# Layer scale on one core: gamma in 16 GpSimd transfers and 16 small matmuls instead of one ScalarE-queue transfer and one matmul

## The chip, the core and the metric

The kernel runs on one core of a Trainium2 chip. The metric is the device time of one execution in microseconds; the figure to compare is the median of several runs. Beside it stands one profiled execution, with a page of readings and a trace that can be asked for more. The kernel is written in Bass: each engine has its own list of instructions, and all order between engines is made by semaphores that the kernel sets and waits for.

## The reference

```python
B, S, D = 1024, 16, 512
x, y: (B, S, D) bfloat16;  gamma: (D,) bfloat16

def reference(x, y, gamma):
    return x + gamma * y
```

The two inputs and the output are 16.8 MB each. Gamma is a single row of 512 numbers, 1 KB, which is applied to every row of y.

## The kernel before, in words

The 16,384 rows of 512 numbers are laid over 128 partitions, 128 consecutive rows to a partition. "Row" below means one of these 128 rows, over all partitions: 1 KB in each partition. All of y stays in SBUF (`y_sb`, 128 rows), and the result is written over it; x has a smaller buffer (`x_sb`, 75 rows), part of which is used twice.

The lists at the top of the file (L6 to L18) are the whole schedule, written by hand:

- `SP` is the list of loads that SyncE issues, in order: y rows 0 to 3, y rows 4 to 63, x rows 0 to 63, y rows 64 to 127, x rows 64 to 116, x rows 117 to 127. The fourth number of an x entry is its place in `x_sb`. Rows 64 to 116 go to the place of rows 0 to 52, so their load has to wait until the add that reads rows 0 to 52 is done (`frees`, L85, and the wait at L107). Rows 117 to 127 need no wait of their own, but stand behind that load in SyncE's list.
- `ACT` is the list of ScalarE's queue: gamma (`'g'`), then the two stores, rows 0 to 63 and rows 64 to 127.
- `EARLY` says that the first two of SyncE's loads are moved to the very start of the program.
- `DVE` is VectorE's order of work on four pieces of 53, 11, 53 and 11 rows: multiply 0, multiply 1, add 0, add 1, multiply 2, multiply 3, add 2, add 3. A multiply (L156) is `y_sb = y_sb * gamma`, an add (L165) is `y_sb = x_sb + y_sb`.

Gamma has to be on all 128 partitions. It is loaded as one row on one partition (`gamma_row`, L56 and L110), a matmul with a row of 128 ones (`ones_row`, L57) as the stationary operand spreads it to 128 partitions in PSUM (`gamma_ps`, L130), and VectorE copies it from there to `gamma_sb` as bfloat16 (L132). TensorE waits for the ones and for gamma ahead of the matmul; VectorE waits for the matmul ahead of the copy, and its first multiply comes after the copy and after y rows 4 to 63 have landed.

TensorE has one more duty: after the matmul it waits for the load of x rows 64 to 116 (`RELEASE`) and then signals `s_go` and `s_rel` (L135 to L137). ScalarE issues the first store only after `s_go`, so the stores begin when that load is in; the first store also needs adds 0 and 1, the second adds 2 and 3. At the end SyncE waits for all stores (L171).

`_take(sem, n, eng)` (L22 to L25) makes an engine wait until a semaphore has reached n and then lowers it by n. Waits that go through it are listed in the profile under L25.

Of the kernel before, what the change touches and what calls it, by code (L numbers as in the profile page):

```python
# [7 lines left out]


SP = [('y', 0, 4), ('y', 4, 64), ('x', 0, 64, 0), ('y', 64, 128), ('x', 64, 117, 0), ('x', 117, 128, 64)]  # L10
ACT = [('g',), ('s', 0, 64), ('s', 64, 128)]

EARLY = (2, 0)

# [7 lines left out]
def _take(sem, n, eng):  # L22


    return eng.wait_ge(sem, n).then_inc(sem, -n)  # L25


def kernel(
# [9 lines left out]
    nc = tc.nc  # L38
# [7 lines left out]
    N, D = xf.shape  # L46
# [4 lines left out]
    dt = xf.dtype  # L51
# [1 line left out]
    yv = yf.rearrange("(p n) d -> p n d", p=P)  # L53
    ov = of.rearrange("(p n) d -> p n d", p=P)

    gamma_row = nc.alloc_sbuf_tensor("gamma_row", [1, D], dt).ap()  # L56
    ones_row = nc.alloc_sbuf_tensor("ones_row", [1, P], dt).ap()  # L57
    gamma_sb = nc.alloc_sbuf_tensor("gamma_sb", [P, D], dt).ap()
    y_sb = nc.alloc_sbuf_tensor("y_sb", [P, rows, D], dt).ap()
    x_loads = [w for w in SP + ACT if w[0] == "x"]  # L60
    y_loads = [w for w in SP + ACT if w[0] == "y"]
    stores = [w for w in SP + ACT if w[0] == "s"]
    for loads in (x_loads, y_loads, stores):
# [3 lines left out]
    gamma_ps = nc.alloc_psum_tensor("gamma_ps", [P, D], mybir.dt.float32).ap()  # L67

    sem = nc.alloc_semaphore
    s_gamma, s_ones, s_ps, s_dve = sem("s_gamma"), sem("s_ones"), sem("s_ps"), sem("s_dve")  # L70
# [8 lines left out]
    def pieces_of(a, b):  # L79
        return [c for c in range(n) if meets(starts[c], starts[c + 1], a, b)]  # L80

    def x_at(row):
        return next(w[3] + row - w[1] for w in x_loads if w[1] <= row < w[2])

    def frees(w):  # L85

        c = set()
        for v in x_loads[: x_loads.index(w)]:
            lo, hi = max(v[3], w[3]), min(v[3] + v[2] - v[1], w[3] + w[2] - w[1])
            if lo < hi:  # L90
                c |= set(pieces_of(v[1] + lo - v[3], v[1] + hi - v[3]))
        return sorted(c)
# [3 lines left out]
    def ring(eng, what, n_early):  # L96

        known, went = 0, False
        for k, w in enumerate(what):
            kind = w[0]  # L100
            need = frees(w) if kind == "x" else pieces_of(w[1], w[2]) + list(w[3:]) if kind == "s" else []
            need = max((order[c] + 1 for c in need), default=0)
            if kind == "s" and not went:
                _take(s_go, 1, eng)
                went = True
            if need > known:
                eng.wait_ge(s_add, need)  # L107
                known = need
            if kind == "g":
                i = eng.dma_start(out=gamma_row, in_=gamma.unsqueeze(0)).then_inc(s_gamma, 16)  # L110
            elif kind == "x":
                to = x_sb[:, w[3] : w[3] + w[2] - w[1], :]
                i = eng.dma_start(out=to, in_=xv[:, w[1] : w[2], :]).then_inc(s_load[w], 16)
            elif kind == "y":
                r = slice(w[1], w[2])
                i = eng.dma_start(out=y_sb[:, r, :], in_=yv[:, r, :]).then_inc(s_load[w], 16)
            else:
                r = slice(w[1], w[2])
                i = eng.dma_start(out=ov[:, r, :], in_=y_sb[:, r, :]).then_inc(s_out, 16)
            if k < n_early:  # L120
                early.append(i.ins)

    ring(nc.sync, SP, EARLY[0])
    ring(nc.scalar, ACT, EARLY[1])


    nc.vector.memset(ones_row, 1.0).then_inc(s_ones, 1)  # L127
    _take(s_ones, 1, nc.tensor)
    _take(s_gamma, 16, nc.tensor)
    nc.tensor.matmul(gamma_ps, ones_row, gamma_row, start=True, stop=True).then_inc(s_ps, 1)  # L130
    _take(s_ps, 1, nc.vector)
    nc.vector.tensor_copy(out=gamma_sb, in_=gamma_ps).then_inc(s_dve, 1)  # L132
    _take(s_dve, 1, nc.vector)
# [16 lines left out]
    for kind, *args in DVE:  # L150
        c = args[0]
        yt = y_sb[:, starts[c] : starts[c + 1], :]
        if kind == "m":
            need(y_loads, c)
            g = gamma_sb[:, None, :].to_broadcast([P, PIECES[c], D])
            nc.vector.tensor_tensor(out=yt, in0=yt, in1=g, op=MULT).then_inc(s_dve, 1)  # L156
            open_mults += 1
        else:
# [4 lines left out]
            at = x_at(starts[c])  # L163
# [46 lines left out]
```

## Time and profile before

| | before |
|---|---|
| median of 3 runs (lowest to highest) | 120.06 us (119.98 to 120.09) |
| profiled execution: span from the first to the last instruction | 118.7 us |
| difference of the median to that span | 1.36 us |
| moved by DMA | 50.33 MB, mean 424 GB/s over the span |
| VectorE busy | 70.0 us, 59% of the span, 10 instructions |
| TensorE busy | 0.6 us, 1 matmul of 577 ns, 1 weight load of 99 ns |
| GpSimd busy | 0.2 us, 4 memsets at the start |
| large multiply or add (53 rows) | 14.29 us each |
| small multiply or add (11 rows) | 3.08 us each |

The trace gives the profiled execution's span and no separate device time for it, so the sums are made against the span of 118.7 us, and the 1.36 us between it and the median are carried over.

How to read it: the engines' busy times don't count the issuing of DMAs, waits and signals; these are seen in the timeline, where a name with a q (SPq, ACTq, PEq) is the sequencer that feeds an engine. A transfer is not in an engine's row at all once it is issued: it is seen in the DMA view, as packets of a queue. Queue q1 holds what SyncE issues, q10 what ScalarE issues. Each of the core's 16 DMA engines works on all the queues.

### The profile page before, as it was taken

The numbers are of one execution on the slowest core, as the hardware profiler recorded it, in microseconds if no ns is written. First come the engines' busy times: TensorE is split into PE (matmuls) and PEld (weight loads), VectorE is DVE, ScalarE is ACT, GpSimd is POOL, SyncE is SP. The second block draws the span as 40 slices with busy tenths as digits, with TensorE's granted clock in tenths as the row PEclk, the third lists the DMA queues.
The fourth block names the chain that finished last, engine by engine and source line by source line (L and its number), as shares of the span: only waits on it lengthen the run. The fifth ranks groups of instructions, "written<-read, shape, count | busy, mean of one in ns | idle before, by whom it ended". The sixth has DMA issues, their size and how long they took to land. (4 is left out here: it accounts for less than half of the span.)

```text
span 118.7 us, 80 instructions
## 1 busy us (share of the span) xinstructions
PE 0.6 (0%) x1; PEld 0.1 (0%) x1; DVE 70.0 (59%) x10; POOL 0.2 (0%) x4
## 2 busy tenths in 40 slices
PE   0001000000000000000000000000000000000000
PEld 0000000000000000000000000000000000000000
DVE  0002000599999299999759999999999910000000
POOL 0000000000000000000000000000000000000000
DMA  8977977998899888998896969498899889988891
GB/s 268 571 332 331 663 331 331 596 464 353 353 486 574 353 353 353 640 420 353 353 585 293 585 293 585 205 634 353 353 596 464 353 353 420 640 353 353 353 663 44
DMA packets 1154, 50.33 MB, mean 424 GB/s; under 512 B 129, under 2 KB 130, under 8 KB 258
## 3 DMA queue, kind: packets, MB, share of 16 engines
q1 hardware_dynamic: 864, 33.55, 66.0%
q10 hardware_dynamic: 290, 16.78, 32.6%
HBM read 33.56 MB, written 16.78 MB: 424 GB/s over the span
## 5 line engine op out<-in xcount | busy, mean ns | idle before, releaser
L156 DVE TENSOR_TENSOR y_sb<-y_sb,gamma_sb 128x27136 bf16<-128x27136 bf16 (+1 forms) x4 | 34.6, 8688 | 12.3 <-DVEq L25 12.3
L165 DVE TENSOR_TENSOR y_sb<-x_sb,y_sb 128x27136 bf16<-128x27136 bf16 (+1 forms) x4 | 34.6, 8689 | 2.3 <-DVEq L25 2.2
L132 DVE CAST gamma_sb<-gamma_ps 128x512 bf16<-128x512 f32 x1 | 0.7, 692 | 8.8 <-DVEq L25 8.8
L127 DVE MEMSET ones_row<- 1x128 bf16 x1 | 0.2, 165 | 2.0 <-PEq L41 2.0
L130 PE MATMUL gamma_ps<-gamma_row,ones_row 1*128 1x512 bf16 x1 | 0.6, 577 | 10.2 <-PEq L25 10.2
L130 PEld LDWEIGHTS gamma_ps<-gamma_row,ones_row 1*128 1x128 bf16 x1 | 0.1, 99 | 10.2 <-issue 10.2
L194 POOL MEMSET const-bfloat16-1.0<- 128x1 bf16 x1 | 0.1, 101 | 0.0
L194 POOL MEMSET const-uint8-127<- 128x1 uint8 x1 | 0.1, 101 | 0.0
L194 POOL MEMSET const-float32-0.0<- 128x1 f32 x1 | 0.1, 98 | 0.2 <-issue 0.2
L194 POOL MEMSET const-float32-1.0<- 128x1 f32 x1 | 0.1, 98 | 0.0
## 6 DMA issues: line engine op xcount, KB each, us to landing
y_sb<-in_y_dram SPq DMA_DIRECT2D x1, 7680.0 KB, 21.4
x_sb<-in_x_dram SPq DMA_DIRECT2D x1, 6784.0 KB, 20.8
x_sb<-in_x_dram SPq DMA_DIRECT2D x1, 1408.0 KB, 23.8
y_sb<-in_y_dram SPq DMA_DIRECT2D x1, 512.0 KB, 3.8
out_dram<-y_sb ACTq DMA_DIRECT2D x2, 22.8
x_sb<-in_x_dram SPq DMA_DIRECT2D x1, 39.3
gamma_row<-in_gamma_dram ACTq DMA_DIRECT2D x1, 1.0 KB
y_sb<-in_y_dram SPq DMA_DIRECT2D x1, 58.3
```

Of the source, the lines that this page charges most:

```text
L127: nc.vector.memset(ones_row, 1.0).then_inc(s_ones, 1)
L130: nc.tensor.matmul(gamma_ps, ones_row, gamma_row, start=True, stop=True).then_inc(s_ps, 1)
L132: nc.vector.tensor_copy(out=gamma_sb, in_=gamma_ps).then_inc(s_dve, 1)
L156: nc.vector.tensor_tensor(out=yt, in0=yt, in1=g, op=MULT).then_inc(s_dve, 1)
L165: nc.vector.tensor_tensor(out=yt, in0=xt, in1=yt, op=ADD).then_inc(s_add, 1)
L194: nc = _bacc.Bacc("TRN2", target_bir_lowering=False, num_devices=1)
```

## The change

Gamma leaves ScalarE's list. GpSimd issues 16 transfers instead, whose lengths are 16 different primes that add up to 512 (`GAMMA`); each has a semaphore of its own, and their destinations lie 96 elements apart in a longer `gamma_row`. GpSimd waits for all 16, signals `s_gamma` once, and then resets the state of these semaphores and clears them. TensorE waits for that one signal and spreads gamma with 16 matmuls, one for each piece, into the matching columns of `gamma_ps`; the last one signals VectorE. All else stays.

```diff
-ACT = [('g',), ('s', 0, 64), ('s', 64, 128)]
+ACT = [('s', 0, 64), ('s', 64, 128)]
+GAMMA = [67, 61, 59, 53, 47, 41, 37, 31, 29, 23, 19, 17, 13, 7, 5, 3]
+APART = 96
...
-    gamma_row = nc.alloc_sbuf_tensor("gamma_row", [1, D], dt).ap()
+    assert sum(GAMMA) == D
+    gamma_row = nc.alloc_sbuf_tensor("gamma_row", [1, len(GAMMA) * APART], dt).ap()
...
-            if kind == "g":
-                i = eng.dma_start(out=gamma_row, in_=gamma.unsqueeze(0)).then_inc(s_gamma, 16)
-            elif kind == "x":
+            if kind == "x":
...
     nc.vector.memset(ones_row, 1.0).then_inc(s_ones, 1)
     _take(s_ones, 1, nc.tensor)
-    _take(s_gamma, 16, nc.tensor)
-    nc.tensor.matmul(gamma_ps, ones_row, gamma_row, start=True, stop=True).then_inc(s_ps, 1)
+    pieces, sems = [], [sem(f"s_gamma_{k}") for k in range(len(GAMMA))]
+    for k, m in enumerate(GAMMA):
+        at = sum(GAMMA[:k])
+        pieces.append((at, m, gamma_row[:, k * APART : k * APART + m]))
+        nc.gpsimd.dma_start(out=pieces[k][2], in_=gamma[at : at + m].unsqueeze(0)).then_inc(sems[k], 16)
+    for s in sems:
+        nc.gpsimd.wait_ge(s, 16)
+    nc.gpsimd.sem_inc(s_gamma, 1)
+    nums = range(sems[0].num, sems[-1].num + 1)
+    assert [s.num for s in sems] == list(nums)
+    nc.gpsimd.dma_reset(nums)
+    nc.gpsimd.sem_clear(nums)
+    _take(s_gamma, 1, nc.tensor)
+    for at, m, piece in pieces:
+        i = nc.tensor.matmul(gamma_ps[:, at : at + m], ones_row, piece, start=True, stop=True)
+    i.then_inc(s_ps, 1)
     _take(s_ps, 1, nc.vector)
     nc.vector.tensor_copy(out=gamma_sb, in_=gamma_ps).then_inc(s_dve, 1)
```

## The prediction

> **What bounds the kernel now.** I read the page first: its row of slices and its queues, and the chain that ended last.
>
> ```profile
> DMA  8977977998899888998896969498899889988891
> q1 hardware_dynamic: 864, 33.55, 66.0%
> q10 hardware_dynamic: 290, 16.78, 32.6%
> HBM read 33.56 MB, written 16.78 MB: 424 GB/s over the span
> ```
>
> The DMA engines are busy in every slice: 50.33 MB at 424 GB/s are 118.7 us, the whole span. Queue 1 is SP's loads, queue 10 is ACT's gamma and stores. The kernel is bound by transfers, and time is lost only if the engines run dry. The chain that ended last is mostly "issue" and says no more, so I went to the timeline, to see which transfer waits for which compute.
>
> ```profile
> 1.91 0.52 ACTq L110 DMA_DIRECT2D gamma_row<-in_gamma_dram  x1
> 10.21 0.10 PEld L130 LDWEIGHTS gamma_ps<-gamma_row,ones_row 1*128 1x128 bf16 x1 [10.21 <-issue]
> 10.24 0.58 PE L130 MATMUL gamma_ps<-gamma_row,ones_row 1*128 1x512 bf16 x1 [10.24 <-PEq L25]
> 10.97 0.69 DVE L132 CAST gamma_sb<-gamma_ps 128x512 bf16<-128x512 f32 x1 [8.81 <-DVEq L25]
> 21.99 17.29 DVE L156 TENSOR_TENSOR y_sb<-y_sb,gamma_sb 128x27136 bf16<-128x27136 bf16 x2 [10.33 <-DVEq L25]
> 41.46 17.29 DVE L165 TENSOR_TENSOR y_sb<-x_sb,y_sb 128x27136 bf16<-128x27136 bf16 x2 [2.17 <-DVEq L25]
> 55.78 0.81 SPq L113 DMA_DIRECT2D x_sb<-in_x_dram  x2
> 60.69 17.29 DVE L156 TENSOR_TENSOR y_sb<-y_sb,gamma_sb 128x27136 bf16<-128x27136 bf16 x2 [1.94 <-DVEq L25]
> 76.95 18.85 ACTq L119 DMA_DIRECT2D out_dram<-y_sb  x2
> 78.13 17.30 DVE L165 TENSOR_TENSOR y_sb<-x_sb,y_sb 128x27136 bf16<-128x27136 bf16 x2
> ```
>
> Gamma is spread by 11.66 us (10.97 + 0.69), and the first multiply starts at 21.99 because y rows 4 to 63 land then. So gamma has 10.3 us to spare. Past that, the first add waits 2.17 us for x. At 55.75 (41.46 + 14.29, one large add) that add frees the space of x rows 64 to 116, and SP issues their load at 55.78. In the answer for 59 to 61 us its first packets move at 59.65, behind y's last ones. A load issued onto free engines moves after about 1.0 us (y's first four rows: issued at 0.00); the first store, beside a load, took up to 2.1 us. I take 1.5, so this load can be issued 59.65 - 55.78 - 1.5 = 2.4 us later for nothing. **Gamma may thus be ready as late as 21.99 + 2.17 + 2.4 = 26.6 us**; each microsecond beyond delays the load, then the release of the stores (which waits for that load), then the end.
>
> Next: why does a 1 KB transfer issued at 1.91 arrive only by 10.2? The DMA view of single microseconds, 7 to 8 and 9 to 10:
>
> ```profile
> DMA packets 17, 0.98 MB, mean 984 GB/s; under 512 B 0, under 2 KB 1, under 8 KB 1
> q1 hardware_dynamic: 16, 0.98, 226.7%
> q10 hardware_dynamic: 1, 0.00, 0.3%
> ...
> DMA packets 12, 0.68 MB, mean 676 GB/s; under 512 B 1, under 2 KB 1, under 8 KB 1
> q1 hardware_dynamic: 11, 0.68, 155.9%
> q10 hardware_dynamic: 1, 0.00, 0.1%
> ```
>
> The loads move in waves of 16 packets, one per engine, each 61,440 bytes (7680 KB in 128 packets); 4 to 5, 6 to 7 and 8 to 9 us start none. Gamma's data goes in the wave of 7 to 8 (narrower stretches: 7.3 to 7.5), its semaphore write only in the next, 9.6 to 9.8. **A small packet of another queue gets one turn after each big packet of the load queue.** A turn costs one wave: 0.983 MB at 430 GB/s (the rate from 22.0 to 41.5) is 2.28 us; the later loads' packets of 65,536 bytes make it 2.44.
>
> **What the Trainium skill says.** "DMA: Bandwidth & Descriptors", section "Queues, rings and completion order": a DMA engine takes turns between its queues packet by packet; the trace agrees, with 2.3 us between the two packets above. Same page, "Why a DMA increments its semaphore by 16 and not by 1": a transfer issued by SP or ACT has only the engines it uses post a semaphore write, but one issued by GpSimd has all 16 engines post one, whatever its shape. For ACT the trace agrees (290 packets = 256 of the stores, their 32 semaphore writes, and 2 of gamma); for GpSimd nothing here shows it. Same page, "Anatomy of one DMA — SWDGE (gpsimd) path": about 2.0 us fixed for each, mostly completion; not shown here.
>
> **The change, part by part.**
>
> Removed: one issue on ACT (0.52 us) and two small packets of one engine (0.3% and 0.1% of 16 engine-microseconds, some 0.06 us). ACT's next work waits until 76.95, so the issue gains nothing; the packets gain 0.06 us at most.
>
> Added on GpSimd: 16 transfers. If each has all 16 engines post, each engine gets 16 semaphore writes and one data packet: **17 packets, 17 turns**. POOL is idle from 0.43 us, the others begin at 1.9, so it starts about when ACT did; its issue time is not in the trace. Bounds: 0.52 us each (ACT's) to 2.0 (the skill's fixed cost, most of it not issue). Either is below a turn of 2.28, so the turns set the pace. I let the first turn be ACT's, at 7.5; a slower start means a wave later. Sixteen more waves: 6 of y (13.7) to 21.2, 10 of 65,536-byte packets (24.4) to 45.6. Bounds: a data packet that brings its semaphore write along saves 2.4; a start one wave later costs 2.4.
>
> Then: the wave's spread over the engines (7.35 to 7.95, so 0.6); from the semaphore write to TensorE's start (9.78 to 10.21, so 0.4); the extra hop over GpSimd with its 16 waits, not shown, 0 to 0.6, I take 0.2; 16 matmuls over the same 512 columns: 0.58 + 15 further weight loads of 0.10 = 2.1 (0.6 if the loads hide, 4 if each pays a start); 0.15 to the copy, 0.69 for it, 0.1 to the multiply. Sum: 4.2. **The first multiply starts at 49.8**.
>
> From there: both multiplies to 67.1 (17.29), the large add to 81.4 (14.29), load issued, first packets at 82.9 (1.5). Before, it was 17.3 us from these packets (59.65) to the release of the stores (76.95), and 41.75 us from there to the end of the span: 100.2 and 141.9. Put shortly, 49.8 - 26.6 = 23.2 us are added to 118.7. Sum against the profiled execution: 118.7 + 23.2 = 141.9 of span, and the 1.36 us by which the median of the runs (120.06) exceeds it gives **143.3 us**. The trace states no own time for its execution beyond the span, so 1.36 also holds what differs between it and the median run.
>
> What queues behind the new waits: on TensorE the release of the stores, due only at 100.2; on DVE every multiply; on SP, behind the delayed load, x rows 117 to 127, which wait for nothing else. What is late next is the second store: the last add ends at 81.4 + 3.1 + 17.3 + 17.3 = 119.1, the first store lands at 100.2 + 22.4 = 122.6; 3.5 us, enough for an issue of up to 2.1.
>
> Costed at nothing: the reset and clearing on GpSimd come after its signal, in some 90 us in which POOL has nothing to do (0.2 us busy in all); without that cover they would cost an estimated 1 us or two at the end. The longer gamma_row and 15 more semaphores occupy no queue.
>
> **The rivals.**
>
> (1) *Few packets per engine: not slower.* If only the engine that carries a piece posts, or if the engines take GpSimd's small packets together in one turn, the issue sets gamma. The sixteenth issue ends between 1.9 + 16 x 0.52 = 10.2 and 1.9 + 16 x 2.0 = 33.9; at 1.0 us each it is 17.9, plus two waves (4.7) and the 4.2: 26.8. That is the deciding point of 26.6, so 120.1 to 121, and no gain below it since y, not gamma, ends that wait. At 2.0 us each it would be 42.8 and 136. For it: the pieces are tiny and each has one engine. Against: the skill's sentence on GpSimd, and the separate turns of gamma's two packets above.
>
> (2) *Two packets per turn.* Half the turns: the ninth at 7.5 + 13.7 + 2 x 2.44 = 26.1, multiply at 30.3, 124 us.
>
> (3) *More packets.* If the pieces go to one engine after all (the change not doing what it says), or every transfer gives each engine a padding packet too, an engine has some 32 turns. The load queue is empty after 59.7 us, as the next load waits for gamma; then small packets pass freely. The cap is 59.7 + 1 + 4.2 = 64.9 for the multiply, 158 us.
>
> A gain is excluded but for the 0.06 us above.
>
> **How the numbers follow.** What a measurement of this kernel can tell from no change is about 0.2%, 0.24 us. My forecast has a chance of 0.68, with its own bounds from 138 to 148; rival 1 has 0.16 (0.06 of it within 0.2%, the rest slower), rival 2 and its neighbours 0.07, rival 3 0.07; 0.02 is left for a gain that I don't see. The range from 123 to 151 holds the forecast, rival 2 from its 124 up, rival 1 with slow issue and a little of rival 3: 8 in 10. Faster 0.02, within 0.2% 0.06, slower 0.92.
>
> **What would show it right or wrong.** The profile after should have a third queue with some 16 x 17 = 272 small packets, one per engine in each wave from about 7.5 to 45 us; TensorE's first matmul at 46 to 47, 16 of them in about 2 us; the first multiply near 50; a hole in the DMA slices from about 60 to 83 us; x's last load issued near 81, stores from 100. Some 32 small packets, or a first matmul before 25 us, make the forecast wrong and rival 1 right; a matmul at 60 or later speaks for rival 3.

## The result, and the profile after

The changed kernel takes **157.34 us** (median of 4 runs, 157.21 to 157.69) against 120.05 us before: the ratio is 1.3105, with a 95% interval from 1.3088 to 1.3122. Its profiled execution took 157.4 us with a span of 156.1 us. The forecast of 143.3 us had the direction right and the size wrong: the measured time is 14 us above it, 6 us above the end of its range (151), and 0.7 us from the 158 us of rival 3.

The page of the kernel after, its row of slices and its queues (packets, MB, share of 16 engines):

```profile
DMA  9969969969799690000000006999796998969966
q1 hardware_dynamic: 864, 33.55, 50.5%
q10 hardware_dynamic: 288, 16.78, 24.8%
q0 software_dynamic: 512, 0.00, 0.2%
```

Two things are new. There is a hole of nine slices in which next to nothing moves, and a queue q0, GpSimd's, with 512 packets that use 0.2% of the engines. The loads and stores are the same packets as before, only later. The timeline of the kernel after (start, length, engine, line) shows who waited:

```profile
2.43 8.31 POOL L136 DMA_DIRECT2D gamma_row<-in_gamma_dram  x16 [1.99 <-POOLq L45]
61.70 0.63 PEld L146 LDWEIGHTS gamma_ps<-gamma_row,ones_row 1*128 1x128 bf16 x16 [61.70 <-issue]
61.73 0.68 PE L146 MATMUL gamma_ps<-gamma_row,ones_row 1*128 1x67 bf16 x16 [61.73 <-PEq L29]
62.56 0.69 DVE L149 CAST gamma_sb<-gamma_ps 128x512 bf16<-128x512 f32 x1 [60.40 <-DVEq L29]
63.62 17.29 DVE L173 TENSOR_TENSOR y_sb<-y_sb,gamma_sb 128x27136 bf16<-128x27136 bf16 x2 [0.37 <-DVEq L29]
81.06 17.29 DVE L182 TENSOR_TENSOR y_sb<-x_sb,y_sb 128x27136 bf16<-128x27136 bf16 x2
95.38 0.80 SPq L116 DMA_DIRECT2D x_sb<-in_x_dram  x2
114.41 18.96 ACTq L122 DMA_DIRECT2D out_dram<-y_sb  x2
```

The first multiply starts at 63.62 instead of 21.99, x's last large load is issued at 95.38 instead of 55.78, and the first store at 114.41 instead of 76.95, which is 37.5 us later; the span is 37.4 us longer. So the whole loss is there by the release of the stores, and nothing after it adds any. The 16 transfers were issued by 10.7 us, and TensorE needed 0.68 us for its 16 matmuls. What is left is the time from issue to landing. The DMA view lists it for each transfer in the order of issue; the last number is microseconds to landing (the first four of 16, and the last):

```profile
gamma_row<-in_gamma_dram POOLq DMA_DIRECT2D x1, 0.1 KB, 8.2
gamma_row<-in_gamma_dram POOLq DMA_DIRECT2D x1, 0.1 KB, 12.1
gamma_row<-in_gamma_dram POOLq DMA_DIRECT2D x1, 0.1 KB, 16.1
gamma_row<-in_gamma_dram POOLq DMA_DIRECT2D x1, 0.1 KB, 18.1
...
gamma_row<-in_gamma_dram POOLq DMA_DIRECT2D x1, 0.0 KB, 51.2
```

Each transfer is issued 0.52 us after the one ahead, and most take about 4 us longer, so they land some 4.5 to 4.8 us apart: two waves of the load queue for each, where the forecast had one. Two of them, the fourth and the ninth, land only some 2.5 us after the one ahead, and the last four nearly together. The DMA view of the kernel after, of 7 to 8 us, then of 21 to 22.5, then of 59.7 to 60.5, says why:

```profile
DMA packets 32, 0.98 MB, mean 983 GB/s; under 512 B 16, under 2 KB 16, under 8 KB 16
q1 hardware_dynamic: 16, 0.98, 227.3%
q0 software_dynamic: 16, 0.00, 0.9%
...
q1 hardware_dynamic: 32, 1.05, 161.8%
q0 software_dynamic: 32, 0.00, 1.2%
...
q0 software_dynamic: 128, 0.00, 9.0%
q1 hardware_dynamic: 16, 0.00, 1.1%
```

In a wave, 16 big packets and 16 small ones start, which is one of each for each of 16 engines (the views don't name a packet's engine; this is read from the counts). At 21 us, where one load ends and the next begins, the load's 16 semaphore writes take a turn as well, and 32 small packets pass. The trace has the same at 40.4 us, at the end of the next load. By 59.7 us only 384 of the 512 are through. Then the load queue is empty, because its next load waits for gamma, and the last 128 pass within 0.8 us. 512 packets over 16 engines and 16 transfers are **two for each engine and transfer**. By their sizes in the trace, 12 are pieces of 34 to 134 bytes, 28 are single numbers of 2 bytes (the four shortest pieces, 13 + 7 + 5 + 3, split number by number), and 472 are of 4 bytes. Of these, 256 would be the semaphore writes of 16 engines for 16 transfers. The other 216 carry no gamma; by their number they stand where an engine has no data.

### The profile page after: what moved, and what is told of

Its sections match the earlier page's. It is cut to its first block, busy times and chain, and to the rows that moved or that the text cites. A ratio compares the mean times of both kernels' runs of the same rounds, so it can differ in the third digit from the quotient of the medians.

```text
span 156.1 us, 135 instructions
## 1 busy us (share of the span) xinstructions
PE 0.7 (0%) x16; PEld 0.6 (0%) x16; DVE 69.9 (45%) x10; POOL 8.5 (5%) x20
## 5 line engine op out<-in xcount | busy, mean ns | idle before, releaser
L149 DVE CAST gamma_sb<-gamma_ps 128x512 bf16<-128x512 f32 x1 | 0.7, 693 | 60.4 <-DVEq L29 60.4
L136 POOL DMA_DIRECT2D gamma_row<-in_gamma_dram x16 | 8.3, 528 | 2.0 <-POOLq L45 2.0
L146 PE MATMUL gamma_ps<-gamma_row,ones_row 1*128 1x67 bf16 (+15 forms) x16 | 0.7, 191 | 61.7 <-PEq L29 61.7
L146 PEld LDWEIGHTS gamma_ps<-gamma_row,ones_row 1*128 1x128 bf16 x16 | 0.6, 107 | 61.7 <-issue 61.7
## 6 DMA issues: line engine op xcount, KB each, us to landing
x_sb<-in_x_dram SPq DMA_DIRECT2D x1, 6784.0 KB, 18.7
```

Of the source, the lines that this page charges most:

```text
L136: nc.gpsimd.dma_start(out=pieces[k][2], in_=gamma[at : at + m].unsqueeze(0)).then_inc(sems[k], 16)
L146: i = nc.tensor.matmul(gamma_ps[:, at : at + m], ones_row, piece, start=True, stop=True)
```

## The experiments

The theory: gamma's lateness is a count of turns. Each transfer by GpSimd gives every engine two packets, each packet waits for one big packet of the load queue, and what passes 26.6 us is added to the kernel's time. Its rivals: the matmuls, GpSimd as issuer, a fixed time for each transfer whatever the loads do, or a queue that is served only when the loads are done.

**The two other parts alone.** First gamma in one transfer by GpSimd, with one matmul:

```diff
-GAMMA = [67, 61, 59, 53, 47, 41, 37, 31, 29, 23, 19, 17, 13, 7, 5, 3]
+GAMMA = [512]
-APART = 96
+APART = 512
```

> Gamma in one transfer by GpSimd and one matmul: the change of the issuing engine alone. Theory: 2 turns, gamma on all engines' count at about 10.4 and spread by 13 us, under the 22 us at which y lands: 120.05 us. If GpSimd's path itself were late, up to 157.

Measured: 119.99 us, ratio 0.9998 (0.9988 to 1.0008). There were 32 packets of q0, and the matmul started at 10.73 instead of 10.24. So GpSimd as issuer and its extra signal cost gamma half a microsecond, which its slack covers, and the kernel nothing.

Then gamma as before by ScalarE's queue, spread by 16 matmuls:

```diff
-ACT = [('s', 0, 64), ('s', 64, 128)]
+ACT = [('g',), ('s', 0, 64), ('s', 64, 128)]
...
-    _take(s_gamma, 1, nc.tensor)
+    _take(s_gamma, 16, nc.tensor)
     for at, m, piece in pieces:
```

GpSimd's transfers, waits and signal are left out.

> Gamma in one transfer by ScalarE's queue as before, spread by 16 matmuls: the matmul part of the change alone. 16 matmuls took 0.68 us after the change against 0.58 for one: gamma spread at about 11.8, 120.05 us under every theory that blames the transfers; more only if the matmuls carried a cost that the trace hides.

Measured: 120.10 us, ratio 1.0009 (1.0002 to 1.0015): within 0.2% of before. The 16 matmuls took 0.68 us and gamma was spread at 11.75.

**The number of transfers.** The same kernel with 4, 6 and 8 pieces; the list changes, and with 4 and 6 pieces also the distance of their places in `gamma_row` (`APART`):

```diff
+GAMMA = [131, 127, 127, 127]
+GAMMA = [83, 83, 83, 83, 83, 97]
+GAMMA = [67, 61, 67, 61, 67, 61, 67, 61]
```

> Gamma in 4 transfers by GpSimd (131, 127, 127, 127 numbers) and 4 matmuls, all else as in the change. Theory (each transfer gives every engine two packets, and each packet waits for one big packet of the load queue): 8 turns per engine, the eighth at 7.5 + 6 x 2.27 + 2.42 = 23.5 us, 0.6 of spread, 1.3 to TensorE, 1.5 to the multiply: it starts at about 26.9, 0.3 past the free limit of 26.6, so 120.4 us; 128 small packets. One packet per transfer: 4 or 5 turns, gamma long before 22, 120.05. A fixed delay of GpSimd's path whatever the number of transfers: as after the change, 157.3.

> Gamma in 6 transfers by GpSimd (five of 83 numbers, one of 97) and 6 matmuls: a third point between 4 and 8. Theory: 192 small packets, 12 turns; from the two runs beside it (first multiply at 24.21 with 8 turns and at 43.44 with 16) four turns of 2.42 less than with 16: 33.8, so 120.05 + 33.8 - 26.6 = 127.2 us. A threshold instead of a slope: 120 or 137.

> Gamma in 8 transfers by GpSimd (67 and 61 numbers in turn) and 8 matmuls. Theory of two packets per engine and transfer: 16 turns, the last at 7.5 + 6 x 2.27 + 9 x 2.42 = 42.9, multiply at about 46.4, so 120.05 + 46.4 - 26.6 = 139.8 us; 256 small packets. One packet per transfer (and one of data per engine): 9 turns, 25.9, multiply at 29.4, 122.9 us. A fixed delay: 157.3.

Measured: 120.04 us, ratio 0.9999 (0.9986 to 1.0013), with 4 pieces; 127.59, ratio 1.0615 (1.0584 to 1.0646), with 6; 137.09, ratio 1.1424 (1.1401 to 1.1446), with 8. The queue and the first multiply in the page and timeline of these three, in that order:

```profile
q0 software_dynamic: 128, 0.00, 0.1%
24.21 17.29 DVE L173 TENSOR_TENSOR y_sb<-y_sb,gamma_sb 128x27136 bf16<-128x27136 bf16 x2 [0.37 <-DVEq L29]
```

```profile
q0 software_dynamic: 192, 0.00, 0.1%
33.81 17.29 DVE L173 TENSOR_TENSOR y_sb<-y_sb,gamma_sb 128x27136 bf16<-128x27136 bf16 x2 [0.37 <-DVEq L29]
```

```profile
q0 software_dynamic: 256, 0.00, 0.1%
43.44 17.29 DVE L173 TENSOR_TENSOR y_sb<-y_sb,gamma_sb 128x27136 bf16<-128x27136 bf16 x2 [0.37 <-DVEq L29]
```

From 4 to 8 pieces each transfer adds 32 packets and (43.44 - 24.21) / 4 = 4.81 us to the multiply's start. Two turns of 2.42 us would be 4.84. With 4 pieces gamma is 2.2 us late for y and the kernel is not slower: there is slack past y. The expected starts for 4 and 8 pieces were 2.7 and 3.0 us too late, about one turn, the one that passes beside a load's semaphore writes at 21 us.

**The price of a turn.** The change with its 16 transfers untouched, and SP's loads in shorter packets, first of 32,768 bytes at most, then of 8,192; the loads of x are changed alike:

```diff
-                i = eng.dma_start(out=y_sb[:, r, :], in_=yv[:, r, :]).then_inc(s_load[w], 16)
+                i = eng.dma_start(out=y_sb[:, r, :], in_=yv[:, r, :], max_dma_last_dim=32768).then_inc(s_load[w], 16)
```

> The change with SP's loads cut into packets of at most 32 KB (half as long, twice as many); gamma's 16 transfers untouched. Theory: a turn costs the big packet ahead of it, now about 1.14 to 1.21 us, and 32 of them take some 37 us instead of running into the end of the load queue: last small packet at 43 to 45, multiply at 46 to 48, 140 us. If each transfer cost GpSimd's path a fixed time of its own, or gamma waited for the load queue to empty whatever its packets, nothing would change: 157.3.

> The change with SP's loads cut into packets of at most 8 KB. Theory: a turn costs about 0.3 us, 32 turns some 10 us, about as fast as GpSimd issues (8.3 us for 16): gamma spread before 22 us and about 120 us, if loads in short packets move as fast as in long ones; if they don't, that shows in y's landing and in the GB/s. Fixed cost per transfer, or waiting for an empty load queue: 157.

Measured: 139.06 us, ratio 1.158 (1.1454 to 1.1706), with packets of up to 32 KB; 122.06, ratio 1.0165 (1.0135 to 1.0194), with 8 KB. The first multiply of the two, and their GpSimd queues:

```profile
q0 software_dynamic: 512, 0.00, 0.2%
45.90 17.29 DVE L173 TENSOR_TENSOR y_sb<-y_sb,gamma_sb 128x27136 bf16<-128x27136 bf16 x2 [0.37 <-DVEq L29]
```

```profile
q0 software_dynamic: 512, 0.00, 0.2%
22.81 17.29 DVE L173 TENSOR_TENSOR y_sb<-y_sb,gamma_sb 128x27136 bf16<-128x27136 bf16 x2 [4.06 <-DVEq L29]
```

The same 512 packets, with packets half as long ahead of them, let the multiply start at 45.9; in the trace the small packets then start 1.14 and later 1.21 us apart, half of before. With 8 KB packets gamma is spread at 18.7 (18.05 + 0.69) and the multiply waits for y again (4.06 us of idle time). So the loads' packet length sets the price of a turn, and the queue is served while loads run. The 8 KB run is still 2.0 us slower than before; its control is the kernel before with such loads.

> The kernel before, with SP's loads cut into packets of at most 8 KB: the control for the run of the change with such loads, which took 122.06 us. If what is left of the loss there is the loads' own (y rows 4 to 63 landed 0.8 us later), this takes 122.0 too; if it is gamma's, 120.05.

Measured: 121.87 us, ratio 1.014 (1.0111 to 1.0169). The intervals of the two overlap, so what was left is, as far as these runs can tell, the shorter packets' own: y rows 4 to 63 let the multiply start at 22.55 there, 0.56 later than before, and the first store went out at 78.80, 1.85 later.

**No big packets at all.** SyncE holds back y rows 4 to 63 and what follows until GpSimd has all 16 transfers:

```diff
-EARLY = (2, 0)
+EARLY = (1, 0)
+            if w == ("y", 4, 64):
+                _take(s_hold, 1, eng)
     nc.gpsimd.sem_inc(s_gamma, 1)
+    nc.gpsimd.sem_inc(s_hold, 1)
```

> The change, with SyncE holding back y rows 4 to 63 and all later loads until GpSimd has seen all 16 transfers: the same 512 small packets without big packets to wait for. Theory: the packets pass as they are issued (last issue ends at 10.7), all are in by 12.7, the held load's first packets move at about 15 instead of 2.8: 120.05 + 12.4 = 132.4 us, 25 less than after the change although every load starts later. If the transfers were slow by themselves, gamma would be late here too, and everything behind it: 157 or more.

Measured: 130.35 us, ratio 1.0845 (1.0814 to 1.0877). From its timeline and its DMA view of the first 20 us (the first two landings):

```profile
11.62 0.68 PE L150 MATMUL gamma_ps<-gamma_row,ones_row 1*128 1x67 bf16 x16 [11.62 <-PEq L29]
32.29 17.29 DVE L177 TENSOR_TENSOR y_sb<-y_sb,gamma_sb 128x27136 bf16<-128x27136 bf16 x2 [19.14 <-DVEq L29]
...
gamma_row<-in_gamma_dram POOLq DMA_DIRECT2D x1, 0.1 KB, 2.0
gamma_row<-in_gamma_dram POOLq DMA_DIRECT2D x1, 0.1 KB, 1.6
```

Without big packets beside them (only y rows 0 to 3, in packets of 4,096 bytes, are loaded at the start), every one of the 16 transfers lands 1.5 to 2.0 us after its issue, near the 2.0 us that the prediction took as the fixed time of a transfer, and all are in before 11.6. Idle engines for 10 us cost less than 32 turns, 130 against 157 us, but more than the kernel before. The expected time was 2 us too long: GpSimd started 0.5 us earlier here (1.96 instead of 2.43), and by the trace all transfers had landed at 11.3, where I had allowed 12.7.

**Another issuer.** ScalarE issues the same 16 transfers ahead of its stores. GpSimd still waits for them, signals and clears the semaphores; only its reset of their state is left out:

```diff
-        nc.gpsimd.dma_start(out=pieces[k][2], in_=gamma[at : at + m].unsqueeze(0)).then_inc(sems[k], 16)
+        nc.scalar.dma_start(out=pieces[k][2], in_=gamma[at : at + m].unsqueeze(0)).then_inc(sems[k], 16)
```

> The change with its 16 transfers issued by ScalarE's queue in place of GpSimd (GpSimd still waits for all and signals). Theory of packets per engine: before, gamma's single transfer left two packets on one engine, so if all 16 go to that same engine, it has 32 turns although the other 15 have next to none; gamma is late by as much as after the change, 157.3 us, with some 32 packets of q10 beside the stores' 288 in place of 512. If instead the transfers go to 16 different engines: 2 turns each, and the issue (16 x 0.52 us) sets gamma: spread by 17 us, 120.05. If GpSimd's own path is what is slow: 120 to 130.

Measured: 157.62 us, ratio 1.3114 (1.3015 to 1.3213). ScalarE's queue and the first multiply:

```profile
q10 hardware_dynamic: 320, 16.78, 24.7%
...
64.22 17.29 DVE L172 TENSOR_TENSOR y_sb<-y_sb,gamma_sb 128x27136 bf16<-128x27136 bf16 x2 [0.37 <-DVEq L29]
```

Here there are only 32 small packets (320 less the stores' 288), a sixteenth of GpSimd's, and the time is that of the change. In the trace they start one after another, mostly one in each wave, data and semaphore write in turn, from 7.5 to 61.0 us. That is how packets in line on one engine would pass; the views don't name the engine, so this is inferred. It leaves the same count for both kernels, 32 on the fullest engine, and the total of small packets doesn't matter.

**Two tries to lower the count.** Each of the 16 transfers asked for as a single packet, and 8 transfers written as 2 x 2 rows of 16 numbers with gaps:

```diff
-        nc.gpsimd.dma_start(out=pieces[k][2], in_=gamma[at : at + m].unsqueeze(0)).then_inc(sems[k], 16)
+        nc.gpsimd.dma_start(out=pieces[k][2], in_=gamma[at : at + m].unsqueeze(0), single_packet=True).then_inc(sems[k], 16)
...
-GAMMA = [67, 61, 59, 53, 47, 41, 37, 31, 29, 23, 19, 17, 13, 7, 5, 3]
+GAMMA = [64] * 8
...
+        nc.gpsimd.dma_start(out=pieces[k][2], in_=gamma[at : at + m].unsqueeze(0).rearrange("p (a b c) -> p a b c", a=2, b=2)).then_inc(sems[k], 16)
```

> The change with every one of the 16 transfers asked for as a single packet. If data (or padding) and semaphore write then pass in one turn: 16 turns, last at 42.9, multiply at 46.9, 140.4 us. If the request changes nothing for transfers this small, 32 turns and 157.3.

> Gamma in 8 transfers of 64 numbers by GpSimd, each written as 2 x 2 rows of 16 with gaps between, so that the transfer counts along more than one dimension. If such a transfer is given to 2 engines without padding for the other 14, an engine has 8 semaphore writes and 2 to 4 data packets: 10 to 12 turns, last at 28.4 to 33.2, multiply at 32 to 37, 125 to 130 us against 139.8 for 8 plain transfers. If every engine gets a padding packet here too, 139.8 or more.

Measured: 157.45 us, ratio 1.3112 (1.3074 to 1.315), and 137.09, ratio 1.1416 (1.1383 to 1.145). The packets of q0 were 512 and 256, as without these edits, and both expectations of a gain failed. In every run with GpSimd the count was 32 per transfer, whatever its shape: 32, 128, 192, 256, 256, 512. So the forecast's 17 packets for 16 transfers by GpSimd did not come about in any run, and the theory is tested by the number and the price of turns alone.

## Why the prediction was wrong, by its own steps

**The count of packets was the step that failed.** The step "16 semaphore writes and one data packet: 17 packets, 17 turns" should have been 32. The first half holds: 512 packets leave room for all 16 engines' posts for each transfer, as the Trainium skill has it ("DMA: Bandwidth & Descriptors", section "Why a DMA increments its semaphore by 16 and not by 1"). The data packet was taken for one engine's alone. In the runs the count is two packets for every engine and transfer, whether the engine has data or not. The bounds of the step, one packet fewer or one wave later, did not reach this. It was put into rival 3 as "a padding packet too" with a chance of 0.07, so the range ended at 151. Rival 3's own sign, a first matmul at 60 us or later, was met: it started at 61.73.

**Seventeen turns would have ended before the loads did; 32 did not.** Thirty-two turns at the forecast's waves would have reached 7.5 + 6 x 2.28 + 25 x 2.44 = 82 us. They were cut off at 59.7, when the load queue ran dry, as rival 3 had it. Its cap of 64.9 for the multiply measured 63.62.

**One turn per big packet, at 2.3 to 2.4 us, was right**, as the views of the waves show and the shorter packets confirm. Missed was that a load's semaphore write also counts as a packet: two small ones passed at 21 and again at 40.4 us, worth two turns. So even with its own count the forecast was too long. Its 17th turn was put at 45.6 us; in the trace of the 16 transfers by ScalarE the 16th and 17th packets both start at 40.5. The run with 8 transfers, which has 16 turns, took 137.09 us, so 17 turns would have taken about 137 and not 143.3 (an estimate). This error made the forecast longer and the wrong count made it shorter; that it lay only 14 us off is in part luck.

**The slack of 26.6 us and the rest of the chain were right in sum.** Adding to 120.05 what the multiply's start in the profiled execution exceeds 26.6 by gives the measured median within 0.4 us:

| kernel | first multiply | 120.05 + (start - 26.6) | measured |
|---|---|---|---|
| 4 transfers | 24.21 | 120.05 (within the slack) | 120.04 |
| 6 transfers | 33.81 | 127.3 | 127.59 |
| 8 transfers | 43.44 | 136.9 | 137.09 |
| 16, loads of 32 KB packets | 45.90 | 139.4 | 139.06 |
| the change | 63.62 | 157.1 | 157.34 |
| 16 by ScalarE | 64.22 | 157.7 | 157.62 |

Two of its terms erred against each other. In the trace after, the first packets of x rows 64 to 116 moved at 96.35, 1.0 us after their issue and not 1.5, and from there to the first store it was 18.1 us and not 17.3.

**Smaller terms.** GpSimd's issue was bounded by 0.52 and 2.0 us and measured 0.52 (8.31 for 16), so it stayed hidden under the turns. The matmuls took 0.68 us against an estimated 2.1, the weight loads being hidden. From the last small packets to TensorE it was 1.3 us against 0.4 + 0.2. The hop over GpSimd is not what was long: the last landing is at 61.4 (issued at 10.2, 51.2 us to landing), 0.3 us ahead of TensorE. The other 1.0 us lies between the start of the last packets and their landing, after the 128 had passed in a burst; in the run that holds the loads back it is 0.3 by its trace. The sum from the last small packets (60.4) to the multiply is 3.2, against 4.2 with the spread of the wave in it. No gain was seen from the issue taken off ScalarE's list, as said. What the reset and clearing would cost without cover, put at 1 us or two, no run shows.

## What to carry to other kernels

In this kernel a small transfer beside bulk loads did not cost its bytes but its turns: packets in line on its fullest DMA engine, times the time of one bulk packet (2.3 to 2.4 us for each of 32, cut off where the loads ended, against 55 ns of work for gamma's two packets before). Splitting the transfer multiplied the turns, by GpSimd's queue as by ScalarE's. Before counting, read from the profile how many packets one transfer leaves in its queue and how many of them start in one wave, and look for the point at which the bulk queue runs dry, for there the lateness is cut off.

## What the hardware showed that was not expected

- A transfer by GpSimd left 32 packets, by the waves two on each of 16 engines; the last four of the change, of 13, 7, 5 and 3 numbers, passed as 128. One by ScalarE left two in all. Sixteen by ScalarE behaved as if all stood on one engine.
- A load's own semaphore writes counted as packets: where they passed, at 21 and 40.4 us, two small packets of an engine passed in place of one.
- By the sizes in the traces, GpSimd split 512 numbers into 16 packets of 64 bytes, left primes from 17 up whole, and cut pieces of 13, 7, 5 and 3 numbers into single numbers of 2 bytes. ScalarE's queue left all of these whole.
- 16 issues took 8.31 us on GpSimd (0.52 each) and 5.12 us on ScalarE (0.32 each).
- The matmuls of 3 to 67 columns have 161 to 233 ns in the profile, yet 16 of them with their weight loads fit into 0.68 us.
- Loads in packets of 8 KB took about 1.7 us more for the whole kernel than in packets of up to 64 KB (121.87 against 120.20 in the same comparison).
